# Block sums of a Fourier transform's matrix, made by accumulating DMAs in place of VectorE

## The chip, the cores and the metric

The kernel runs on one core of a Trainium2 chip. The metric is the device time in microseconds of one execution. Before the change, three runs took 742.9, 743.92 and 747.85 us; their median is 743.92 us.

The core has a matrix engine (TensorE, PE in the profile, with its weight loads as PEld), a vector engine (VectorE, DVE), an engine for activation functions (ScalarE, ACT), a programmable engine (GpSimd, POOL) and SyncE (SP), which here only issues transfers. The engines run side by side, each through its own list of instructions in order, and wait for each other by semaphores. 16 DMA engines move data between the memory of the chip (HBM) and the core's own memory (SBUF, 128 partitions). TensorE accumulates in PSUM.

## The reference

`x` has 2048 rows (the sequence) of 512 values. The output mixes two branches of it by a gate per row:

```python
g = sigmoid((x * gate_w).sum(-1, keepdims=True))
# A: real part of a Fourier transform over both axes
a = x @ dft_hid_re.T;  b = x @ dft_hid_im.T
A = dft_seq_re @ a - dft_seq_im @ b
# B: gated feed-forward layer, F = 1376
B = (silu(x @ w1) * (x @ w3)) @ w2
out = g * A + (1 - g) * B
```

All is float32. The Fourier matrices come as inputs, as any matrix would.

## The kernel before

**Products.** A float32 product is three passes on TensorE: each operand is split into a high part (rounded) and a low part (the rest), and high x high, high x low and low x high are accumulated (`mm3`, L85). The split is made by `split` (L76): ScalarE writes the high part by a copy (L77), VectorE the low part by a subtraction (L83). Each operand that comes from memory or from a sum passes through it.

**Stages.** The feed-forward branch comes first, up to 339 us of the profile. Then the transform along the sequence, Z = (C x) by blocks, up to 652 us, which spills Z to HBM. Then the product with the hidden matrix, the gate and the sum.

**The sequence transform** is a product of 2 x 2 blocks by 2 x 2 blocks, made in seven products and some sums (Winograd's form of Strassen's algorithm). The fixed operand `A` is made from `x` once (`load_a`, L414 to L433): blocks and sums of blocks, split, in `A1` and `A2`. The moving operand is the matrix C, which is streamed from HBM (`cc`): for each of four column groups `tb` and each of eight pairs `p` of row tiles, four blocks of 128 x 512 floats, which the host has laid side by side. C needs four blocks as they are and sums of blocks.

The work is a list of 64 steps `(tb, g, p)` (L435). For each `tb` there are eight steps with g = 0, of four products each, and then eight with g = 1, of three products each. Each product of a step is six matmuls of 128 x 512. In a step:

- `load_c(n + 4)` (L438) asks SyncE for the blocks of the step four later. For g = 0 it loads blocks 0 and 1 into a wide buffer `cu` and block 2 into half of a wide buffer `cv`; for g = 1 blocks 2 and 3 into `cu`, block 1 into half of `cv`.
- `sums_c(n + 2)` makes two sums on VectorE, 128 x 512 each. For g = 0: T1 = block 2 - block 0 (L469), T2 = block 1 - T1 (L470). T2 stays in a half buffer, because the same pair p needs it again in g = 1. For g = 1: block 1 - block 2 (L472), and block 3 - T2 (L473).
- `prep_c1(n + 2)` splits the wide buffer `cu`, `prep_c2(n + 2)` the sums (T1 and T2 for g = 0, the last sum for g = 1), into `zo`, of which there are four buffers.
- Six or eight accumulators in PSUM are carried over the eight steps; after the last of them VectorE adds them up (L556 to L590) and the result is spilled.

The wide buffers (`wide`, L73) come from one pool `f4` of 13, which loads of all stages share. SyncE's queue issues all these loads in order, each when its buffer has been read to the end. The lines of code call the helpers in an order written out by hand; the framework's scheduler then sets each engine's order from the dependences, so that the lists of the engines are not always in the order of the code. The first steps' loads and preparations are called from the end of the feed-forward stage (`xacts`, L500 to L517).

After the transform, the last two of the four tiles of the hidden matrix are split with their sign turned (`load_d`, `neg=True`, L79).

Of the kernel before, what the change touches and what calls it, by code (L numbers as in the profile page):

```python
# [7 lines left out]
F32 = mybir.dt.float32  # L8
F32R = mybir.dt.float32r
AF = mybir.ActivationFunctionType  # L10
ALU = mybir.AluOpType

P = 128
# [15 lines left out]
def fnet_swiglu_gate_kernel(  # L29
# [11 lines left out]
):  # L41
    """A float32 product is three passes: each operand v is split exactly into
    hi = v rounded to 12 significant bits and lo = v - hi, and hi*hi + hi*lo +
    lo*hi is accumulated in float32.

    The gate and up products are one 2x2x2 block product (gate | up weights by
    halves of D by two token blocks) in the seven products of Winograd's form of
    Strassen's algorithm, and so is the transform along the sequence (halves of
    D by halves of the sequence by re | im)."""
    nc = tc.nc  # L50
# [24 lines left out]

    def split(hi, lo, src, neg=False):  # L76
        nc.scalar.activation(hi, src, AF.Copy, scale=-1.0 if neg else 1.0)  # L77
        if neg:
            nc.vector.scalar_tensor_tensor(  # L79
                lo, src, -1.0, hi.bitcast(F32), op0=ALU.mult, op1=ALU.subtract  # L80
            )
        else:
            nc.vector.tensor_sub(lo, src, hi.bitcast(F32))  # L83

# [11 lines left out]

# [1 line left out]
    XO, ST = {}, {}  # L98

    def load_xo(g, t, j):  # L100
        """Half j of the staged operands t of token blocks 2g and 2g+1."""
        if g not in ST:
            ST[g] = [[wide(f"xs{g}_{q}_{i}") for i in range(4)] for q in range(2)]
            XO[g] = [xo.tile([P, 2, 7, 512], F32R, tag="xo", name=f"xo{g}_{q}") for q in range(2)]
        for q in range(2):
            nc.sync.dma_start(ST[g][q][t][:, j * 512 : (j + 1) * 512],
                              xt[g, q, :, t * 1024 + j * 512 : t * 1024 + (j + 1) * 512])

    # moving operands B11 B21 B22 T1 T2 T3 -T4 and where they are staged
    AT = {"B12": (0, 0), "B11": (0, 1), "B21": (1, 0), "B22": (1, 1),  # L110
# [29 lines left out]
    def prep_wa(i, lo=0, hi=3):  # L140
        """A11 A12 A22"""
        if lo == 0:
            WA[i] = wo.tile([P, 2, 3, 256], F32R, tag="wa", name=f"wa{i}", bufs=LOOK + 1)
        t = WA[i]
        split(t[:, 0, lo:hi].rearrange("p a n -> p (a n)"),
              t[:, 1, lo:hi].rearrange("p a n -> p (a n)"),
              WS[i][:, lo:hi].rearrange("p a n -> p (a n)"))

    def prep_wb(i, part=None):
        """S1 S2 S3 S4"""  # L150
        if part != 1:
            w = WS.pop(i)
            u = wo.tile([P, 4, 256], F32, tag="wu", name=f"wu{i}", bufs=1)
            nc.vector.tensor_add(u[:, 0], w[:, 3], w[:, 2])
            nc.vector.tensor_sub(u[:, 1], u[:, 0], w[:, 0])
            nc.vector.tensor_sub(u[:, 2], w[:, 0], w[:, 3])
            nc.vector.tensor_sub(u[:, 3], w[:, 1], u[:, 1])
            WB[i] = u
        if part != 0:
            u = WB[i]  # L160
            t = wo.tile([P, 2, 4, 256], F32R, tag="wb", name=f"wb{i}")
            split(t[:, 0].rearrange("p a n -> p (a n)"), t[:, 1].rearrange("p a n -> p (a n)"),
                  u.rearrange("p a n -> p (a n)"))
            WB[i] = t
# [19 lines left out]
    def first2(i):  # L184
        """the gate of the first block is P1 + P2"""
        y = bank(4 + i % 2, f"Y{i}")
        prod(y, i, 1, 1, True)
        s1 = G[i][1]
        nc.vector.tensor_add(s1, s1, y)
        nc.scalar.activation(s1, s1, AF.Silu)  # L190
# [90 lines left out]
    def plain(b12, a21):  # L281
        """The first chunk in eight products: they need no sums."""
        c = {}

        def half(i, j, w, x, start):
            if start:
                c[i, j] = bank((0, 4, 6, 7)[2 * i + j], f"C{i}{j}")
            for r in range(2):
                sl = slice(r * P, (r + 1) * P)
                mm3(c[i, j], w(0, sl), w(1, sl), x(r, 0), x(r, 1), start and r == 0,  # L290
                    not start and r == 1)

        def wa(k):
            return lambda h, sl: WA[0][:, h, k, sl]

        def xb(k):
            return lambda q, h: XO[0][q][:, h, k, :]

        w21 = lambda h, sl: a21[:, h, sl]
        x12 = lambda q, h: b12[:, h, q * 512 : (q + 1) * 512]  # L300
        s1 = tp.tile([P, 512], F32, tag="s1", name="s1_0", bufs=LOOK + 2)
        g1 = tp.tile([P, 512], F32, tag="g1", name="g1_0")
        h = wide("h0")
        H[0] = h
        yield half(0, 0, wa(0), xb(0), True)
        yield half(1, 0, w21, xb(0), True)
        half(0, 0, wa(1), xb(1), False)
        nc.scalar.activation(s1, c[0, 0], AF.Silu)
        yield half(1, 0, wa(2), xb(1), False)
        nc.vector.tensor_mul(h[:, :512], s1, c[1, 0])  # L310
        half(0, 1, wa(0), x12, True)
        yield half(1, 1, w21, x12, True)
        half(0, 1, wa(1), xb(2), False)
        nc.scalar.activation(g1, c[0, 1], AF.Silu)
        half(1, 1, wa(2), xb(2), False)
        yield nc.vector.tensor_mul(h[:, 512:], g1, c[1, 1])
# [91 lines left out]

# [1 line left out]
    # rows d (halves) by [re | im] columns t, reduced over s (halves)  # L410
    a2_cm, a2 = pool("a2", 1, "left")
# [8 lines left out]
    def load_a(p):  # L420
        """A11 S1 S2 S4 | A12 A22 S3 of the rows s of tiles p and p + 8."""
        r = wide(f"xr{p}").rearrange("p (a n) -> p a n", a=4)
        m = wide(f"xm{p}").rearrange("p (a n) -> p a n", a=4)
        nc.sync.dma_start(flat(r), xn[p])
        a21, a11, a12, a22 = (r[:, i] for i in range(4))
        nc.vector.tensor_add(m[:, 0], a21, a22)
        nc.vector.tensor_sub(m[:, 1], m[:, 0], a11)
        nc.vector.tensor_sub(m[:, 2], a12, m[:, 1])
        nc.vector.tensor_sub(m[:, 3], a11, a21)
# [5 lines left out]
    steps = [(tb, g, p) for tb in range(NTB) for g in range(2) for p in range(NG)]  # L435
    RAW, T2, ZO = {}, {}, {}

    def load_c(n):  # L438
        if n >= len(steps):
            return  # L440
        tb, g, p = steps[n]
        u, v = wide(f"cu{n}"), wide(f"cv{n}")
        src = cc[tb, p]
        if g == 0:
            nc.sync.dma_start(u, src[:, :1024])
            nc.sync.dma_start(v[:, :512], src[:, 1024:1536])
        else:
            nc.sync.dma_start(u, src[:, 1024:])
            nc.sync.dma_start(v[:, :512], src[:, 512:1024])
        RAW[n] = u, v  # L450

# [8 lines left out]

    def sums_c(n):
        if n >= len(steps):
            return
        tb, g, p = steps[n]
        u, v = RAW[n]
        if g == 0:
            b11, b22 = u[:, :512], u[:, 512:]
            T2[tb, p] = v[:, 512:] if p % 2 == 0 else RAW[n - 1][1][:, :512]
            nc.vector.tensor_sub(v[:, :512], v[:, :512], b11)  # L469
            nc.vector.tensor_sub(T2[tb, p], b22, v[:, :512])  # L470
        else:
            nc.vector.tensor_sub(u[:, :512], v[:, :512], u[:, :512])  # L472
            nc.vector.tensor_sub(v[:, 512:], u[:, 512:], T2.pop((tb, p)))  # L473

    def prep_c1(n):
        if n < len(steps):
            zsplit(n, 0, RAW[n][0])

    def prep_c2(n):
        if n >= len(steps):  # L480
            return
        tb, g, p = steps[n]
        v = RAW[n][1]
        if g == 1:
            zsplit(n, 1, v[:, 512:])
        elif p % 2 == 0:
            zsplit(n, 1, v)
        else:
            zsplit(n, 1, v[:, :512], T2[tb, p])

# [10 lines left out]
    for p in range(NG):  # L501
        xacts[p].append(lambda p=p: load_a(p))
    xacts[7].append(lambda: load_c(0))
    xacts[8].append(lambda: load_c(1))
    xacts[9].append(lambda: prep_c1(0))
    xacts[10].append(lambda: sums_c(0))
    xacts[10].append(lambda: prep_c2(0))
# [5 lines left out]
    prep_c1(1)  # L513
    sums_c(1)
    prep_c2(1)
    load_c(2)
    load_c(3)  # L517

# [5 lines left out]
    def fourier_step(n):  # L524
        tb, g, p = steps[n]
        fst, lst = p == 0, p == NG - 1
        load_c(n + 4)
        sums_c(n + 2)
        z0, z1 = ZO.pop((n, 0)), ZO.pop((n, 1))
# [64 lines left out]

# [1 line left out]
    DW, ZY = [], {}  # L596

    def load_d(q):
        r = wide(f"dr{q}")
        nc.sync.dma_start(r, dd[q])  # L600
        t = yd.tile([P, 2, 1024], F32R, tag=f"d{q}", name=f"d{q}")
        split(t[:, 0], t[:, 1], r, neg=q >= 2)
        DW.append(t)
# [113 lines left out]
```

## Time and profile before

| | before |
|---|---|
| median of three runs | 743.92 us |
| span of the profiled execution, first to last instruction | 742.8 us |
| matmuls | 3196 |
| sequence transform, matmuls | 339 to 652 us |
| DMA moved | 112.5 MB, mean 151 GB/s |
| HBM read, written | 95.16 MB, 16.78 MB |
| transfers of the moving operand | 64 of 512 KB and 64 of 256 KB |

The time outside the span isn't listed for the profiled execution; its span lies at the lowest of the three times.

How to read the lines that follow. A row of a group of instructions names line, engine and operation, then output <- inputs with their shape and the count, then the busy time in us and the mean ns of one, and behind the second bar the idle time of that engine just before these instructions with what ended it. A row of a wait says which engine's instruction waited for what, with the total in us, the number of times and the longest. A row of a tile gives the shortest, median and longest duration in ns, and the time of the first and the last one. In the timeline a row begins with its start and length in us.

### The profile page before, as it was taken

What the parts mean: (1) busy time and instruction counts of PE and PEld (TensorE: products, weight loads), DVE (VectorE), ACT (ScalarE), POOL (GpSimd) and SP (SyncE); (2) the same over time, 40 slices, a digit from 0 to 9 for tenths busy, and PEclk for the clock granted to TensorE, in tenths of its full rate; (3) what the DMA queues carried; (4) which work ended last, traced back from release to release, by engine and by line L of the source; (5) the groups of instructions that cost most, each with busy time, mean ns of one, the idle gap of its engine ahead of it and who ended that gap; (6) DMA issues with size and microseconds to landing.
All of it is one profiled execution on the core that took longest, in us unless ns stands there. A gap on an engine that the chain in (4) does not pass through costs nothing.

```text
span 742.8 us, 8637 instructions
## 1 busy us (share of the span) xinstructions
PE 731.3 (98%) x3196; PEld 597.6 (80%) x3196; DVE 541.0 (73%) x793; ACT 336.5 (45%) x455; POOL 0.2 (0%) x4
## 2 busy tenths in 40 slices
PE   8999999999999999999999899999999999999998
PEld 5788888888888888888887688878887788888886
DVE  6997788792777668994986887779776978834331
ACT  6755463554554436753443344344343445523320
POOL 0000000000000000000000000000000000000000
PEclk9999999999999999999999999999999999999999
DMA  7112126532013003608656554655465647963331
GB/s 268 51 65 85 57 75 248 163 124 114 30 56 114 1 28 113 210 32 313 225 172 224 197 182 146 220 189 203 153 213 172 217 163 244 350 241 114 114 107 63
DMA packets 40378, 112.50 MB, mean 151 GB/s; under 512 B 4368, under 2 KB 4752, under 8 KB 40336
## 3 DMA queue, kind: packets, MB, share of 16 engines
q1 hardware_dynamic: 38032, 107.89, 42.1%
q10 hardware_dynamic: 2304, 4.06, 1.5%
q8 instruction: 25, 0.41, 0.2%
q14 instruction: 17, 0.14, 0.1%
HBM read 95.16 MB, written 16.78 MB: 151 GB/s over the span
## 4 chain that ended last, share of the span: by engine, by line
PE 82%; DVE 8%; DMA 8%; issue 1%; ACT 1%; SPq 0%; DVEq 0%; ACTq 0%
PE P L87 26%; PE acc L87 16%; PE X L87 16%; PE y L87 12%; PE Z L87 8%; DMA cv<-cc 7%; DVE zo L83 5%; PE Y L87 4%; PE C L87 1%; DVE cv L469 1%; DMA xs<-xt 1%; DVE cv L470 1%; DVE zu L583 1%; DMA cu<-cc 1%; DVE zu L584 0%
## 5 line engine op out<-in xcount | busy, mean ns | idle before, releaser
L87 PE MATMUL P<-zo,a 128*128 128x512 f32 x1344 | 307.7, 390 | 5.6 <-DVE zo L83 4.8
L87 PEld LDWEIGHTS P<-zo,a 128*128 128x128 f32 x1344 | 251.4, 188 | 61.8 <-DVE zo L83 7.6
L87 PE MATMUL acc<-w2o,ho 128*128 128x512 f32 x528 | 120.1, 389 | 0.0
L77 ACT ACTIVATE zo<-cu 128x1024 fp32r<-128x1024 f32 x64 | 67.9, 1060 | 111.9 <-PE P L87 82.8
L87 PEld LDWEIGHTS acc<-w2o,ho 128*128 128x128 f32 x528 | 99.1, 188 | 20.7
L87 PE MATMUL X<-xo,wb 128*128 128x512 f32 x378 | 93.8, 390 | 0.0
L87 PE MATMUL y<-d,zy 128*128 128x512 f32 x384 | 87.2, 389 | 0.0
L87 PEld LDWEIGHTS y<-d,zy 128*128 128x128 f32 x384 | 72.1, 188 | 15.0
L77 ACT ACTIVATE zo<-cv 128x512 fp32r<-128x512 f32 (+1 forms) x80 | 56.2, 715 | 61.7 <-PE P L87 50.8
L87 PEld LDWEIGHTS X<-xo,wb 128*128 128x128 f32 x378 | 70.6, 188 | 15.6 <-DVE u L206 0.5
L83 DVE TENSOR_TENSOR zo<-cu,zo 128x1024 fp32r<-128x1024 f32 x64 | 78.2, 1222 | 2.6 <-ACT zo L77 2.5
L83 DVE TENSOR_TENSOR zo<-cv,zo 128x512 fp32r<-128x512 f32 (+1 forms) x80 | 62.3, 796 | 4.0 <-ACT zo L77 4.0
L83 DVE TENSOR_TENSOR zy<-zr,zy 128x1024 fp32r<-128x1024 f32 x16 | 19.5, 1225 | 40.6 <-ACT zy L77 36.3
L469 DVE TENSOR_TENSOR cv<-cv,cu 128x512 f32<-128x512 f32 x32 | 21.8, 694 | 33.6 <-DMA cv<-cc 33.6
L77 ACT ACTIVATE zy<-zr 128x1024 fp32r<-128x1024 f32 x16 | 16.8, 1056 | 44.7 <-PE y L87 43.1
L77 ACT ACTIVATE wa<-ws 128x768 fp32r<-128x768 f32 (+2 forms) x23 | 18.8, 818 | 33.6 <-PE Z L87 32.0
L87 PE MATMUL X<-xo,wa 128*128 128x512 f32 x126 | 32.7, 391 | 0.0
L87 PE MATMUL Y<-xo,wa 128*128 128x512 f32 x126 | 32.5, 389 | 0.0
L87 PE MATMUL Z<-xo,wb 128*128 128x512 f32 x126 | 32.3, 389 | 0.0
L87 PE MATMUL Z<-xo,wa 128*128 128x512 f32 x126 | 32.2, 389 | 0.0
L83 DVE TENSOR_TENSOR wb<-wu,wb 128x1024 fp32r<-128x1024 f32 x21 | 25.7, 1225 | 8.2 <-ACT wb L77 8.1
L472 DVE TENSOR_TENSOR cu<-cv,cu 128x512 f32<-128x512 f32 x32 | 22.1, 691 | 12.6 <-DMA cv<-cc 11.1
(84 smaller groups left out, 661.2 us busy)
## 6 DMA issues: line engine op xcount, KB each, us to landing
cu<-cc SPq DMA_DIRECT2D x64, 512.0 KB, 4.5
cv<-cc SPq DMA_DIRECT2D x64, 256.0 KB, 3.8
ws<-w SPq DMA_DIRECT2D x21, 512.0 KB, 3.2
zr<-zsp SPq DMA_DIRECT2D x16, 512.0 KB, 6.0
w2r<-w SPq DMA_DIRECT2D x10, 512.0 KB, 4.1
xs<-xt SPq DMA_DIRECT2D x16, 256.0 KB, 5.3
sr<-xs SPq DMA_DIRECT2D x8, 512.0 KB, 4.2
bsp<-b SPq DMA_DIRECT2D x8, 512.0 KB, 3.0
```

Source lines behind the costliest of these rows:

```text
L77: nc.scalar.activation(hi, src, AF.Copy, scale=-1.0 if neg else 1.0)
L83: nc.vector.tensor_sub(lo, src, hi.bitcast(F32))
L87: nc.tensor.matmul(ps, u, v, start=first and n == 0, stop=last and n == 2, skip_group_check=chain)
L469: nc.vector.tensor_sub(v[:, :512], v[:, :512], b11)
L470: nc.vector.tensor_sub(T2[tb, p], b22, v[:, :512])
L472: nc.vector.tensor_sub(u[:, :512], v[:, :512], u[:, :512])
L583: nc.vector.tensor_add(u4[:, r], u4[:, r], U["P7"][r])
```

## The change

The four sums of a pair p are no longer made by VectorE. GpSimd's queue issues DMAs that add what they read to what lies at their destination (`add_dma`). The sums are all additions now: T1 = block 2 + block 0, T2 = block 1 + T1, then block 2 + block 1 and block 3 + T2. That is the transform with the sign of two blocks turned; the sums of `A` in `load_a` follow, and the hidden matrix is split without turning a sign.

- T1 and T2 get wide buffers of their own, each shared by an even and an odd p (`pairs`). For g = 0 SyncE loads blocks 0 and 1 into `cu`, block 2 into T1 and block 1 into T2. Then an accumulating DMA adds block 0 from HBM to T1, and another adds T1 to T2 from SBUF to SBUF; this second one is called a step later.
- For g = 1 SyncE loads blocks 2 and 3 into `cu`, and that is all. Accumulating DMAs add block 1 to the first half of `cu`, and block 3 to T2, which has lain there since g = 0.
- `add_c(n + 4)` issues these just behind `load_c(n + 4)`. The third step's load and adds are called earlier than before, in the last chunk of the stage ahead.
- What the host hands over is the same.

```diff
@@ load_a
-        nc.vector.tensor_add(m[:, 0], a21, a22)
-        nc.vector.tensor_sub(m[:, 1], m[:, 0], a11)
-        nc.vector.tensor_sub(m[:, 2], a12, m[:, 1])
+        nc.vector.tensor_sub(m[:, 0], a22, a21)
+        for d, v, w in ((1, m[:, 0], a11), (2, a12, m[:, 1])):
+            nc.vector.scalar_tensor_tensor(m[:, d], v, -1.0, w, op0=ALU.mult, op1=ALU.subtract)
@@ new
+    def add_dma(dst, src):
+        nc.gpsimd.dma_start(dst, src, accum_op=ALU.add)
+
+    def pairs(tb, p, src):
+        if p % 2 == 0:
+            T1[tb, p // 2] = wide(f"t1_{tb}_{p}")
+            T2[tb, p // 2] = wide(f"t2_{tb}_{p}")
+        h = slice(p % 2 * 512, p % 2 * 512 + 512)
+        nc.sync.dma_start(T1[tb, p // 2][:, h], src[:, 1024:1536])
+        nc.sync.dma_start(T2[tb, p // 2][:, h], src[:, 512:1024])
@@ load_c
-        u, v = wide(f"cu{n}"), wide(f"cv{n}")
+        u = RAW[n] = wide(f"cu{n}")
         src = cc[tb, p]
         if g == 0:
             nc.sync.dma_start(u, src[:, :1024])
-            nc.sync.dma_start(v[:, :512], src[:, 1024:1536])
+            pairs(tb, p, src)
         else:
             nc.sync.dma_start(u, src[:, 1024:])
-            nc.sync.dma_start(v[:, :512], src[:, 512:1024])
@@ in place of sums_c
-        if g == 0:
-            b11, b22 = u[:, :512], u[:, 512:]
-            T2[tb, p] = v[:, 512:] if p % 2 == 0 else RAW[n - 1][1][:, :512]
-            nc.vector.tensor_sub(v[:, :512], v[:, :512], b11)
-            nc.vector.tensor_sub(T2[tb, p], b22, v[:, :512])
-        else:
-            nc.vector.tensor_sub(u[:, :512], v[:, :512], u[:, :512])
-            nc.vector.tensor_sub(v[:, 512:], u[:, 512:], T2.pop((tb, p)))
+    def add_c(n):
+        if n < len(steps):
+            tb, g, p = steps[n]
+            src = cc[tb, p]
+            if g == 0:
+                add_dma(half(T1, tb, p), src[:, :512])
+            else:
+                add_dma(RAW[n][:, :512], src[:, 512:1024])
+                add_dma(half(T2, tb, p), src[:, 1536:])
+        if 0 < n <= len(steps) and steps[n - 1][1] == 0:
+            tb, g, p = steps[n - 1]
+            add_dma(half(T2, tb, p), half(T1, tb, p))
@@ prep_c2
-        v = RAW[n][1]
-        if g == 1:
-            zsplit(n, 1, v[:, 512:])
-        elif p % 2 == 0:
-            zsplit(n, 1, v)
+        if g == 0:
+            zsplit(n, 1, half(T1, tb, p), half(T2, tb, p))
         else:
-            zsplit(n, 1, v[:, :512], T2[tb, p])
+            zsplit(n, 1, half(T2, tb, p))
@@ first steps, called from the stage ahead
     xacts[7].append(lambda: load_c(0))
+    xacts[7].append(lambda: add_c(0))
     xacts[8].append(lambda: load_c(1))
+    xacts[8].append(lambda: add_c(1))
     xacts[9].append(lambda: prep_c1(0))
-    xacts[10].append(lambda: sums_c(0))
+    xacts[10].append(lambda: load_c(2))
+    xacts[10].append(lambda: add_c(2))
     xacts[10].append(lambda: prep_c2(0))
...
     prep_c1(1)
-    sums_c(1)
+    load_c(3)
+    add_c(3)
     prep_c2(1)
-    load_c(2)
-    load_c(3)
@@ fourier_step
         load_c(n + 4)
-        sums_c(n + 2)
+        add_c(n + 4)
@@ load_d
-        split(t[:, 0], t[:, 1], r, neg=q >= 2)
+        split(t[:, 0], t[:, 1], r)
```

More of the change, by code (lines that the diff above doesn't have):

```diff
@@ L74, in wide, with split @@
         return f4.tile([P, 1024], F32, tag="f4", name=name)
[L76 to L81, printed above, removed]
-        else:
-            nc.vector.tensor_sub(lo, src, hi.bitcast(F32))
+    def split(hi, lo, src):
+        nc.scalar.activation(hi, src, AF.Copy)
+        nc.vector.tensor_sub(lo, src, hi.bitcast(F32))
     def mm3(ps, ah, al, bh, bl, first, last, chain=False):
@@ L435, in fnet_swiglu_gate_kernel, with half @@
     steps = [(tb, g, p) for tb in range(NTB) for g in range(2) for p in range(NG)]
-    RAW, T2, ZO = {}, {}, {}
+    RAW, T1, T2, ZO = {}, {}, {}, {}
+    def add_dma(dst, src):
[7 more added lines that the diff above has]
+        nc.sync.dma_start(T2[tb, p // 2][:, h], src[:, 512:1024])
+    def half(t, tb, p):
+        return t[tb, p // 2][:, p % 2 * 512 : p % 2 * 512 + 512]
     def load_c(n):
@@ L445, in load_c @@
             nc.sync.dma_start(u, src[:, :1024])
-            nc.sync.dma_start(v[:, :512], src[:, 1024:1536])
+            pairs(tb, p, src)
         else:
             nc.sync.dma_start(u, src[:, 1024:])
-            nc.sync.dma_start(v[:, :512], src[:, 512:1024])
-        RAW[n] = u, v
+    def add_c(n):
[10 more added lines that the diff above has]
+            add_dma(half(T2, tb, p), half(T1, tb, p))
     def zsplit(n, i, *srcs):
@@ L459, in zsplit @@
         ZO[n, i] = t
[L461 to L465, printed above, removed]
-        if g == 0:
-            b11, b22 = u[:, :512], u[:, 512:]
-            T2[tb, p] = v[:, 512:] if p % 2 == 0 else RAW[n - 1][1][:, :512]
[L469 to L473, printed above, removed]
     def prep_c1(n):
         if n < len(steps):
-            zsplit(n, 0, RAW[n][0])
+            zsplit(n, 0, RAW.pop(n))
     def prep_c2(n):
```

## The prediction

> **What bounds the kernel now.** I read the busy shares first, then the windows of the stage that the change touches, then its waits, then the DMA side.
>
> The busy shares of the page:
>
> ```profile
> span 742.8 us, 8637 instructions
> ...
> PE 731.3 (98%) x3196; PEld 597.6 (80%) x3196; DVE 541.0 (73%) x793; ACT 336.5 (45%) x455; POOL 0.2 (0%) x4
> ```
>
> TensorE has work for 98% of the span; VectorE is busy, but not the bound, and GpSimd does nothing. The change lies in the sequence transform. Its matmuls run from 338.9 to 652.1 us (first and last row of the chain in order of time that belong to it, and the row after):
>
> ```profile
> 338.89 10.94 PE P L87 x48
> ...
> 577.66 74.41 PE P L87 x327
> 652.07 87.05 PE y L87 x384
> ```
>
> Its loads and splits run from 309.4 to about 645 (instructions on the buffer `cu`):
>
> ```profile
> L83 DVE TENSOR_TENSOR zo<-cu,zo x64: 1216/1221/1243, 322.2 to 644.8; 128x1024 fp32r<-128x1024 f32 x64
> L445 SPq DMA_DIRECT2D cu<-cc x32: 327/328/737, 309.4 to 581.2; - x32
> ```
>
> The windows view gives both stretches, and the stretch where the DMA engines were fullest (columns: stretch, length, then busy time and count for PE, PEld, DVE, ACT, POOL, then granted clock, mean busy share of the 16 DMA engines, GB/s):
>
> ```profile
> 309.00:645.00 336.00, 330.40 (x1446) 270.26 (x1445) 269.81 (x361) 149.19 (x181) 0.00 (x0) 1.00 0.58 198
> 631.00:650.00 19.00, 19.00 (x85) 15.73 (x85) 16.44 (x20) 11.37 (x14) 0.00 (x0) 1.00 0.91 347
> 339.00:652.00 313.00, 307.40 (x1345) 251.24 (x1344) 248.72 (x326) 132.38 (x156) 0.00 (x0) 1.00 0.61 210
> ```
>
> In the stage PE is idle for 313.0 - 307.4 = 5.6 us. That is all that any relief of VectorE can give back here. Who ends these gaps, by the waits of PE and of its weight loads in the stretch 338 to 653 (columns: total us, times, longest):
>
> ```profile
> PE P L87 <- DVE zo L83: 4.8, 6, 1.2
> PE P L87 <- DVE zu L584: 0.8, 3, 0.3
> ```
>
> The late thing is the low part of a split matrix block, made on VectorE. VectorE in turn waits for a load, and the load for a buffer (waits of all engines, then SyncE's queue):
>
> ```profile
> DVE cv L469 <- DMA cv<-cc: 33.6, 16, 7.7
> ```
>
> ```profile
> SPq L449 <- DVE zo L83: 68.1, 30, 4.6
> SPq L446 <- DVE zo L83: 61.7, 24, 6.5
> ```
>
> One such gap in the timeline:
>
> ```profile
> 413.07 0.69 DVE L469 TENSOR_TENSOR cv<-cv,cu 128x512 f32<-128x512 f32 x1 [3.12 <-DMA cv<-cc]
> ...
> 413.68 1.22 DVE L83 TENSOR_TENSOR zo<-cu,zo 128x1024 fp32r<-128x1024 f32 x1
> 414.81 0.68 DVE L83 TENSOR_TENSOR zo<-cv,zo 128x512 fp32r<-128x512 f32 x1
> 414.93 0.33 SPq L446 DMA_DIRECT2D cv<-cc  x1
> 414.95 5.77 PEld L87 LDWEIGHTS P<-zo,a 128*128 128x128 f32 x26 [1.59 <-DVE zo L83]
> ```
>
> VectorE sat 3.12 us until the load had landed, then did the sum and two splits, and TensorE's weight load, 1.59 us late, started as the last split ended. So the short gaps come where VectorE and the buffers are late together.
>
> **What is removed.** Each pair of blocks costs four sums. Two rows from the page, two from the groups by line:
>
> ```profile
> L469 DVE TENSOR_TENSOR cv<-cv,cu 128x512 f32<-128x512 f32 x32 | 21.8, 694 | 33.6 <-DMA cv<-cc 33.6
> ...
> L472 DVE TENSOR_TENSOR cu<-cv,cu 128x512 f32<-128x512 f32 x32 | 22.1, 691 | 12.6 <-DMA cv<-cc 11.1
> ```
>
> ```profile
> L473 DVE TENSOR_TENSOR cv<-cu,cv 128x512 f32<-128x512 f32 x32 | 22.1, 690 | 7.2 <-DMA cu<-cc 6.7
> L470 DVE TENSOR_TENSOR cv<-cu,cv 128x512 f32<-128x512 f32 x32 | 22.0, 691 | 0.3
> ```
>
> 128 instructions of 0.69 us leave VectorE: 88 us of its 269.8 in the stretch. On the path that sets the end this is worth at most the 5.6 us of gaps, because TensorE covers the rest.
>
> **What is small.** In the first half of the steps the second operand is now always split in two pieces, where for the 16 even steps it was one wide piece:
>
> ```profile
> L77 ACT ACTIVATE zo<-cv x80: 610/633/1064, 326.4 to 643.9; 128x512 fp32r<-128x512 f32 x64, 128x1024 fp32r<-128x1024 f32 x16
> L83 DVE TENSOR_TENSOR zo<-cv,zo x80: 682/688/1230, 327.5 to 646.0; 128x512 fp32r<-128x512 f32 x64, 128x1024 fp32r<-128x1024 f32 x16
> ```
>
> That is 16 times 2 x 633 - 1064 = 0.2 us on ACT and 16 times 2 x 688 - 1230 = 0.15 us on VectorE, 3.2 and 2.3 us under TensorE's cover; if the cover went, at most 5.5 us. The turned signs replace additions by subtractions, or by a two-operation form, of the same size: nothing. SyncE issues as many loads as before, 128: a step of the first half has three in place of two, one of the second half one in place of two, with the same bytes.
>
> **What is added.** 128 accumulating DMAs of 128 x 512 floats (262,144 bytes) on GpSimd's queue, 33.6 MB in all. 96 read the matrix, so 25.2 MB more come from HBM; 32 add one block sum in SBUF to another. No accumulating transfer and no DMA of GpSimd's stands in the trace, so its price has to be bounded.
>
> First the room. In the stretch 309 to 645 the DMA engines are busy for 0.58 x 336 = 195 us at 198 GB/s, which is 66.5 MB, or 341 GB/s while busy. Room up to a full share: 336 - 195 = 141 us, or 141 / 128 = 1.10 us for each accumulating DMA. At the fullest that a row shows, 0.91, it is 0.91 x 336 - 195 = 111 us, 0.87 us for each.
>
> Then the price of one, in time of all 16 engines. A plain transfer of this size takes 262,144 B / 341 GB/s = 0.77 us. The lower end is this price: the second read hides. The upper end is twice it, 1.54 us: an accumulate reads two blocks and writes one, and if reading sets the pace, it takes twice as long. In between, three passes over the data in place of two would give 1.15 us. I take 1.15: it counts every pass of the data once, and I have no row that says that reading alone sets the pace.
>
> The sum by that price: 195 + 128 x 1.15 = 342 us of DMA work. At a share of 0.91 this takes 342 / 0.91 = 376 us, where the stretch had 336: 40 us more. The old gaps are inside the 336, so nothing is to be subtracted. 742.8 + 40 = 783 us for the profiled span. The three runs took 742.9 to 747.85 us; the span lies at the lowest of them and 1.1 us under their median of 743.92, so I forecast 784.
>
> The ends by the same sum: at 0.77 us, 195 + 98 = 293 us, 0.87 of the stretch, and nothing is lost; at 1.15 us and a full share 342 us, 6 us lost; at 1.54 us 392 us, 56 us lost at a full share and 392 / 0.91 - 336 = 95 us at 0.91.
>
> A rule that speaks against this change: the Trainium skill, DMA: Bandwidth & Descriptors, section Issuing engines are not separate DMA queues, says that DMAs of ScalarE, SyncE and GpSimd run on the same 16 engines and interleave. No row of this trace shows two of these queues under load together; if GpSimd's transfers had engines of their own, the sum would be no loss and at most the 5.6 us of gain.
>
> **The new waits.** Landing times, and what an issue costs its queue:
>
> ```profile
> cu<-cc SPq DMA_DIRECT2D x64, 512.0 KB, 4.5
> cv<-cc SPq DMA_DIRECT2D x64, 256.0 KB, 3.8
> ```
>
> ```profile
> L446 SPq DMA_DIRECT2D cv<-cc x32: 327/328/1516, 310.7 to 581.8; - x32
> ...
> DMA to landing us min/median/max: 3.0/3.8/8.7
> ```
>
> A block of the first half is now a chain: load, add, add, three landings. At the median it takes 4.5 + 3.8 + 3.8 = 12.1 us. A step is 24 products of about 0.228 us (row below), 5.5 us, or 18 products, 4.1 us. Loads are asked for four steps ahead, 16 to 22 us, so 12.1 us fit; three landings at the worst row's 8.7 us, 26 us, don't.
>
> ```profile
> 421.42 58.79 PE L87 MATMUL P<-zo,a 128*128 128x512 f32 x258 [0.28 <-DVE zu L584]
> ```
>
> GpSimd's queue is in order. Adding the first block sum to the second waits on it for the first to land, and the adds of the next pair of steps stand behind. An add for the second half waits for VectorE's split of the same buffer, with the next blocks' adds behind it. What waits in turn are ScalarE's splits of these blocks, then VectorE's, then TensorE. Before, the second half loaded two buffers a step; now one, the other lying there already. So with the same 13 buffers the loads may run further ahead, which speaks for the latency being hidden, and for engine time being what is left.
>
> **The rivals.**
>
> Hidden: the accumulates cost about the plain price. The DMA engines then stand at 0.87, below the 0.91 that was reached without a stall, and VectorE's relief takes away some of the gaps. 743.9 - 5.6 = 738.3 us if all go; 742 if the later chain leaves most of them. For it: the 141 us of room, and the gaps ending on VectorE. Against it: any price above 0.87 to 1.10 us ends it. This is the one on the other side; the price per transfer decides, at 1.10 us.
>
> Twice: reading sets the pace, 1.54 us each, 56 to 95 us lost, 800 to 839 us. For it: nothing in the trace shows a second read to be free. Against: the rows show no engine's read and write sides apart. The Trainium skill, Collectives: The Full Stack, section The bandwidth ceiling, says that an add in the DMA path needs two source reads on one ring and so halves the rate; no run here shows that.
>
> GpSimd's queue: the issue on it, not the transfer, sets the pace. A block of 512 columns takes 8 x 5.5 + 8 x 4.1 = 77 us and has 32 accumulates and, in the first half, up to 8 exposed landings of 3.8 us, 30 us. That leaves 47 / 32 = 1.45 us for each issue. SyncE's usual 0.33 us is far below, its longest 1.52 us just above: 32 x 1.52 + 30 = 79 us, 2 us over a block, 8 us in four, 752. An issue of 3 us would give 126 us a block and 940 us; nothing in the trace excludes it, since GpSimd issued nothing.
>
> **How the numbers follow.** Three passes (about 752 to 799, forecast 784): 0.37. Hidden, with the small loss of 6 us at a full share (737 to 751): 0.33. Twice (800 to 840): 0.20. GpSimd's queue, a little over the limit: 0.04 inside the range, and 0.06 far above. The forecast's own range is 750 to 799; with cases of both signs the range is 737 to 839, with some 0.1 left out, nearly all above. About 1% (7.4 us) is what a measurement of this kernel can tell from no change. Faster by over 1% needs below 736.5, which is more than the 5.6 us of gaps: 0.05, for gaps that the records don't show. Within 1%: the rest of the hidden case, 0.28. Slower: the other three, 0.67.
>
> **What would show it.** The four sum groups gone and VectorE near 455 us; a new queue with 33.6 MB and a share of 16 engines: its share of the span over 128 is the price, and 1.15 us each would be 147 us of 784, about 19%. A DMA share near 0.9 throughout the stage; PE idle for some 40 us, the wait before it ending on ScalarE's or VectorE's splits, and these on accumulating DMAs; clock unchanged at 1.00. The forecast is wrong if that queue's share gives 0.8 us or less each (hidden) or 1.5 (twice), or if the DMA engines are far below 0.9 while GpSimd's queue is never empty (issue or landing sets the pace).

## The result, and the profile after

The changed kernel takes 792.36 us (median of four runs, 787.92 to 795.74) against 745.13 us for the kernel before, run beside it (four runs, 742.9 to 747.85). The ratio is 1.063, with a 95% interval of 1.060 to 1.066. The forecast was 784 us with a range of 737 to 839. The profiled execution took 792.24 us, with a span of 790.4.

The page of the changed kernel: busy shares, two rows of the 40 slices, and the DMA queues (packets, MB, share of the 16 engines over the span).

```profile
span 790.4 us, 8944 instructions
...
PE 747.8 (95%) x3196; PEld 604.7 (77%) x3196; DVE 465.2 (59%) x681; ACT 333.7 (42%) x471; POOL 112.6 (14%) x132
...
PEclk9999999999999999998899999989999899999999
DMA  7111146440130036899999999999999999973321
...
q1 hardware_dynamic: 38032, 107.89, 38.9%
q0 software_dynamic: 18432, 33.56, 24.5%
```

VectorE has lost 541.0 - 465.2 = 75.8 us of work, as the sums are gone. A new queue has moved 33.56 MB, and its packets took 24.5% of 790.4 us, 193.7 us; for one of the 128 accumulating DMAs that is 1.51 us of all 16 engines. From about 336 us, where the stage's matmuls begin, to about 690 the DMA row stands at 9. The packets of SyncE's queue (q1) took 38.9% x 790.4 = 307 us; before, for the same 107.89 MB, they took 42.1% x 742.8 = 313 us:

```profile
q1 hardware_dynamic: 38032, 107.89, 42.1%
```

So a packet isn't recorded as longer because the engines are fuller, and the shares can be added up as work. The windows view of the same stretch as before, as far as it now reaches:

```profile
309.00:690.00 381.00, 344.96 (x1436) 275.67 (x1436) 194.04 (x248) 145.09 (x195) 112.38 (x128) 0.96 1.01 264
```

The DMA share is 1.01 over 381 us, where it was 0.58 over 336. (A value above 1 means that the recorded times of packets on one engine overlap, so 1 is no sharp end.) The granted clock is 0.96, where it was 1.00. Two rows for the stage's matmuls, before and after, from the groups of PE by line: busy, mean ns of one, and the idle time before them.

```profile
L87 PE MATMUL P<-zo,a 128*128 128x512 f32 x1344 | 307.7, 390 | 5.6 <-DVE zo L83 4.8 <-DVE zu L584 0.8
```

```profile
L82 PE MATMUL P<-zo,a 128*128 128x512 f32 x1344 | 324.2, 402 | 35.5 <-ACT zo L77 17.4 <-DVE zu L593 11.3 <-DVE zo L78 6.6
```

Idle time grew by 29.9 us, and the same 1344 matmuls took 16.5 us longer: 46.4 of the 47.6 us by which the span grew. A clock of 0.96 over 381 us is 15 us of clock lost, so the slower matmuls are the clock. The waits of all engines after, those that lead from TensorE to the DMAs:

```profile
ACT zo L77 <- DMA t<-t: 75.2, 20, 9.2
...
ACT zo L77 <- DMA cu<-cc: 33.3, 9, 5.8
...
ACT zo L77 <- DMA t<-cc: 23.9, 9, 8.0
```

TensorE waits for ScalarE's split, and ScalarE for a landing, most of all for the last link of the chain, T2 + T1. The 11.3 us that end on VectorE's line 593, a sum at the end of a block, lead there too: before the wait that ends at 612.35 us, VectorE had itself stood 6.77 us for ScalarE's part of a split, and ScalarE 7.72 us for T2 + T1 to land. The landings themselves (issues on SyncE's and GpSimd's queue, median us to landing):

```profile
cu<-cc SPq DMA_DIRECT2D x64, 512.0 KB, 8.3
t<-cc SPq DMA_DIRECT2D x64, 256.0 KB, 8.7
t<-cc POOLq DMA_DIRECT2D x64, 256.0 KB, 7.4
...
t<-t POOLq DMA_DIRECT2D x32, 256.0 KB, 7.1
```

A load that landed in 4.5 us before now takes 8.3. Two readings are possible. The DMA engines are full, and the landings are late because of that ("engine time"). Or the chain of three landings and GpSimd's queue, in order, are what is slow, and the high share only goes along with it ("queue and chain").

### The profile page after: what moved, and what is told of

Same layout as the page of the kernel before. It is cut to its first block, busy times and chain, and to the rows that moved or that the text cites. A ratio compares the mean times of both kernels' runs of the same rounds, so it can differ in the third digit from the quotient of the medians.

```text
span 790.4 us, 8944 instructions
## 1 busy us (share of the span) xinstructions
PE 747.8 (95%) x3196; PEld 604.7 (77%) x3196; DVE 465.2 (59%) x681; ACT 333.7 (42%) x471; POOL 112.6 (14%) x132
## 3 DMA queue, kind: packets, MB, share of 16 engines
q1 hardware_dynamic: 38032, 107.89, 38.9%
q0 software_dynamic: 18432, 33.56, 24.5%
HBM read 120.32 MB, written 16.78 MB: 173 GB/s over the span
## 4 chain that ended last, share of the span: by engine, by line
PE 48%; DMA 27%; issue 12%; POOL 6%; DVE 5%; ACT 1%; POOLq 0%; SPq 0%; DVEq 0%; ACTq 0%
DMA t<-cc 15%; PE X L82 15%; PE y L82 11%; PE acc L82 8%; PE Z L82 7%; DMA cu<-cc 5%; POOL t L436 5%; DMA t<-t 4%; PE Y L82 4%; PE P L82 2%; DMA zr<-zsp 2%; POOL cu L436 2%; DVE a L78 1%; PE C L82 1%; ACT zo L77 1%
## 5 line engine op out<-in xcount | busy, mean ns | idle before, releaser
L82 PE MATMUL P<-zo,a 128*128 128x512 f32 x1344 | 324.2, 402 | 35.5 <-ACT zo L77 17.4
L82 PEld LDWEIGHTS P<-zo,a 128*128 128x128 f32 x1344 | 258.8, 194 | 100.8 <-ACT zo L77 21.7
L436 POOL DMA_DIRECT2D t<-cc x64 | 60.4, 964 | 421.0 <-ACT a L77 315.4
L78 DVE TENSOR_TENSOR zo<-t,zo 128x512 fp32r<-128x512 f32 x96 | 64.7, 687 | 92.0 <-ACT zo L77 92.0
L77 ACT ACTIVATE zo<-t 128x512 fp32r<-128x512 f32 x96 | 58.9, 625 | 118.4 <-DMA t<-t 75.2
L436 POOL DMA_DIRECT2D t<-t x32 | 28.6, 893 | 95.1 <-DMA t<-cc 57.1
L436 POOL DMA_DIRECT2D cu<-cc x32 | 27.9, 872 | 50.9 <-issue 46.6
```

Source lines behind the costliest of these rows:

```text
L77: nc.scalar.activation(hi, src, AF.Copy)
L82: nc.tensor.matmul(ps, u, v, start=first and n == 0, stop=last and n == 2, skip_group_check=chain)
L436: nc.gpsimd.dma_start(dst, src, accum_op=ALU.add)
```

## The experiments

The medians of the kernel before on the same chips were 744 to 746 us. "In the stage" below is the stretch from 309 us to the end of the splits.

**Plain copies in place of the accumulating ones.** The order of instructions is that of the changed kernel on every engine.

```diff
-        nc.gpsimd.dma_start(dst, src, accum_op=ALU.add)
+        nc.gpsimd.dma_start(dst, src)
```

> The changed kernel with plain copies on GpSimd's queue in place of the 128 accumulating ones: same number, same blocks, same waits, and no sum is made. Engine time (an accumulate takes 193.7 / 128 = 1.51 us of all 16 engines, a plain one about 0.77, and the engines are full): 195 + 98 = 293 us fit into the stage, 738 to 750 us, and the software queue's share falls from 24.5% to about 13%. Queue and chain (GpSimd waits in order for landings, three in a row): the waits stay, 770 to 792 us.

Measured: 741.77 us, one run, beside 746.01 for the kernel before. Windows of the stage, the stage's matmuls and the queue:

```profile
309.00:640.00 331.00, 327.95 (x1441) 269.87 (x1440) 194.81 (x248) 149.45 (x197) 69.11 (x128) 1.00 0.92 308
```

```profile
L82 PE MATMUL P<-zo,a 128*128 128x512 f32 x1344 | 306.6, 390 | 3.1 <-ACT zo L77 2.3 <-DVE zo L78 0.7
```

```profile
q0 software_dynamic: 10240, 33.56, 14.2%
```

With the same number of DMAs, the same bytes written and the same order of waits, but without the addition and the second read, 50 us are gone. One plain copy takes 14.2% x 740.0 / 128 = 0.82 us. The DMA share is 0.92, and TensorE idles for 3.1 us. HBM isn't the limit: as much is read from it as in the changed kernel (120.32 MB), and in the stage 308 GB/s are moved where the changed kernel moved 264. Queue and chain aren't cleared by this run alone: a plain copy takes GpSimd 0.54 us to issue, an accumulate 0.87, the queue has 10240 packets in place of 18432, and the chain's landings are shorter too, 6.3 + 6.7 + 5.5 = 18.5 us at the medians.

**Half and three quarters of the columns.** The accumulating DMAs keep their number and their order (but for two early in GpSimd's queue that change places) and move fewer bytes.

```diff
-        nc.gpsimd.dma_start(dst, src, accum_op=ALU.add)
+        nc.gpsimd.dma_start(dst[:, :256], src[:, :256], accum_op=ALU.add)
```

> The changed kernel with each accumulating DMA cut to its first 256 of 512 columns, so that half of each sum is left out: same number, same waits, half the bytes. Engine time: 195 + 128 x 0.76 = 292 us, fits, 738 to 752 us. Queue and chain: 128 issues and all waits remain and landings get only a little shorter, 768 to 790 us.

> The changed kernel with each accumulating DMA cut to 384 of its 512 columns, so that a quarter of each sum is left out; the order of every engine is the same. Engine time: between 0.87 us (256 columns) and 1.51 us (512) lies 1.19 us; work in the stage 304 us of the run with plain copies + 128 x (1.19 - 0.82) = 352 us, at the full share of 1.01 348 us where that run took 331: 742 + 17 = 759 us, 750 to 765. Queue and chain: the waits are nearly those of the changed kernel, 770 to 785 us.

Measured: 742.23 us with 256 columns (one run, beside 746.01), 767.73 us with 384 (ratio 1.032 to the kernel before, 1.028 to 1.037). The queue of each, and the window of the stage with 256 columns:

```profile
q0 software_dynamic: 18432, 16.79, 15.0%
```

```profile
q0 software_dynamic: 18432, 25.17, 20.4%
```

```profile
309.00:640.00 331.00, 326.47 (x1436) 268.99 (x1435) 194.33 (x248) 148.83 (x197) 112.67 (x128) 1.00 0.95 256
```

Both have the 18432 packets of the changed kernel, and GpSimd takes as long to issue (with 256 columns 112.67 / 128 = 0.88 us each). So neither the issue nor the number of packets makes the loss. One DMA takes 15.0% x 740.5 / 128 = 0.87 us with 256 columns, 20.4% x 765.1 / 128 = 1.22 with 384, and 1.51 with 512: it goes mostly by the bytes, half of them costing 0.58 as much, and not by the number of DMAs or packets. The time with 384 columns lies between the two expectations, 3 us above the range of the one and 2 under that of the other, so it decides less than the half did. Its queue took 156 us of all engines, less than the 168 us of the run with 96 accumulates below, and it cost as much.

**Only the first half's DMAs accumulate, only the second half's, or all but T2 + T1.** The others are plain copies; again the order of all engines is that of the changed kernel.

```diff
-    def add_dma(dst, src):
-        nc.gpsimd.dma_start(dst, src, accum_op=ALU.add)
+    def add_dma(dst, src, **kw):
+        nc.gpsimd.dma_start(dst, src, **kw)
...
-                add_dma(half(T1, tb, p), src[:, :512])
+                add_dma(half(T1, tb, p), src[:, :512], accum_op=ALU.add)
...
-            add_dma(half(T2, tb, p), half(T1, tb, p))
+            add_dma(half(T2, tb, p), half(T1, tb, p), accum_op=ALU.add)
```

> The changed kernel with its 64 accumulating DMAs of the first half (T1 and T2, the chain of three landings) as they are, and plain copies in place of the 64 of the second half, whose sums are left out; same order on every engine. Engine time: 304 + 64 x 0.69 = 348 us of work, 345 us at a share of 1.01, 331 before: 756 us, 745 to 762, and the same as with only the second half accumulating. Queue and chain: the chain of three is whole, 775 to 790 us.

> The changed kernel with only the 64 accumulating DMAs of the second half, and plain copies in place of the chain's 64 in the first half, whose sums are left out; same order on every engine. Engine time: 756 us, 745 to 762, as with only the first half accumulating. Queue and chain: no chain of accumulates, 740 to 746 us.

> The changed kernel with plain copies in place of only the 32 DMAs that add T1 to T2 in SBUF, so that this sum is left out; 96 accumulate, same order on every engine. Engine time: 304 + 96 x 0.69 = 370 us of work, 367 us at a share of 1.01, 331 before: 742 + 36 = 778 us, 765 to 785. Against the run with this sum on VectorE (796.6 us with 96 accumulates) it tells what VectorE's waiting in its own order cost there. Queue and chain: the waits of the chain stay, 780 to 792 us.

Measured, with the ratio to the kernel before and its interval, and the share and the idle time of the stage's matmuls from the profiles:

| accumulating, of 128 | us | ratio | DMA share in the stage | PE idle, us |
|---|---|---|---|---|
| none | 741.77 | one run | 0.92 | 3.1 |
| 64, second half | 746.47 | 1.002 (1.000 to 1.004) | 0.99 | 7.0 |
| 64, first half | 749.42 | 1.007 (1.005 to 1.010) | 0.98 | 9.2 |
| 96, all but T2 + T1 | 765.44 | 1.028 (1.023 to 1.032) | 1.01 | 17.1 |
| 128 | 792.36 | 1.063 (1.060 to 1.066) | 1.01 | 35.5 |

The share and the idle time are those of one execution each. For the first half's 64 that was the slowest of six, 753.95 us, so its 9.2 us are on the high side.

64 accumulates bring the share to about 1, with 5 to 8 us lost against the one run with none; each 32 more then cost 16 to 19 and 27 us. Which half accumulates matters by 3 us only, though the intervals don't overlap. With the first half's the chain is as long as in the changed kernel, 7.5 + 8.2 + 7.4 = 23.1 us at the medians, and 8 us are lost where the changed kernel loses 51, so queue and chain as the main cause falls. The 3 us needn't be the chain: a step of the first half also loads four blocks in 5.5 us, one of the second half two in 4.1. And the last 32 are the chain's last link, so part of the 27 us may be the chain's; no run separates that. Engine time had the shape, not the sizes: it gave 756, 756 and 778 us, and the loss sets in later and grows faster. If a plain copy takes 0.82 us, the queues' shares leave 1.39 to 1.48 us for an accumulate in these three mixed runs. That plain copies and accumulates fill the engines in the proportion of 0.82 to 1.51 and that 1.01 is the end is thus good for the place of the limit within some 10 us, no better.

**A source in SBUF.** Blocks 0 and 3 are added from `cu`, where they lie already.

```diff
-                add_dma(half(T1, tb, p), src[:, :512])
+                add_dma(half(T1, tb, p), RAW[n][:, :512])
...
-                add_dma(half(T2, tb, p), src[:, 1536:])
+                add_dma(half(T2, tb, p), RAW[n][:, 512:])
```

> The changed kernel with blocks 0 and 3 added from the buffer cu in SBUF, where they lie already, in place of HBM: 64 of the 96 accumulates that read HBM read SBUF, 16.8 MB less from HBM. Engine time by passes over the data: the engines move the same, 780 to 795 us. If HBM reads are what costs: 745 to 770 us. Queue and chain: the adds wait for cu as well, 788 to 800 us.

Measured: 838.97 us, one run, beside a median of 746.34: slower than any theory had it. The queue, and the largest waits of SyncE's queue in this stage:

```profile
q0 software_dynamic: 18432, 33.56, 22.8%
```

```profile
SPq L460 <- DMA t<-cu: 76.5, 18, 10.1
...
SPq L460 <- DMA t<-t: 39.9, 8, 7.3
```

One accumulate takes 22.8% x 837.2 / 128 = 1.49 us, as with HBM for a source, while the reads from HBM fell from 120.32 to 103.55 MB; so reading HBM isn't what makes it dear. What is new is that a load waits until an accumulate has read the buffer that it is to fill. Here the queue and the buffers do cost: the DMA share in the stage falls to 0.92, and TensorE idles for 66.2 us.

**DMAs beside the kernel before.** Two DMAs in each step, into four buffers that no product reads, accumulating or plain.

```diff
+            nc.gpsimd.tensor_copy(x[:, :1], z[:, 1, :1].bitcast(F32))
+            nc.gpsimd.dma_start(x, cc[tb, p][:, k * 512 : k * 512 + 512], accum_op=ALU.add)
```

> The kernel before, with its sums on VectorE, and beside them two accumulating DMAs of 128 x 512 from HBM in each of the 64 steps, into four buffers that nothing else reads, paced by a small copy on GpSimd from the step's operand. Nobody waits for their landing but the next use of the same buffer, two steps later. Engine time: 195 + 193 = 388 us of DMA work where the stretch had 336, 785 to 800 us. Queue and chain: no product waits for these, 744 to 752 us.

> As the run with the accumulating DMAs beside the kernel before, but plain copies. Engine time: 195 + 98 = 293 us, 0.87 of the stretch, 744 to 752 us. Queue and chain: 744 to 752 us as well. It shows what the four extra DMA buffers, the small copies and the issue on GpSimd cost without the second read.

Measured: 823.85 us accumulating, 787.44 plain, one run each, beside 746.01. The control lost 41 us, against both theories, so the pair doesn't tell what it should. The small copy that paces the DMAs reads the split operand, and it made that buffer's next user wait (the kernel with plain copies):

```profile
ACT zo L77 <- POOL xe L520: 14.8, 5, 4.9
```

That covers only a part of the 41 us. The loads landed later, 5.8 and 5.0 us at the median where the kernel before has 4.5 and 3.8, and VectorE's sums wait for them; that this is the rest wasn't tested. The queues' shares give 13.5% x 785.6 / 128 = 0.83 us for a plain copy and 24.0% x 822.1 / 128 = 1.54 us for an accumulate, the prices of the other runs, and 36 us lie between the two.

**T2 + T1 on VectorE.** 96 accumulating DMAs remain.

```diff
-            add_dma(half(T2, tb, p), half(T1, tb, p))
+            nc.vector.tensor_add(half(T2, tb, p), half(T2, tb, p), half(T1, tb, p))
```

> The changed kernel with the sum T2 + T1 (32 DMAs from SBUF to SBUF) back on VectorE as 32 additions; 96 accumulating DMAs remain and the chain of three landings becomes one of two. Engine time: 195 + 96 x 1.51 = 340 us where 336 were, 4 us over, 744 to 760 us. Queue and chain: 64 accumulates of the second half and 32 of the first still pass GpSimd's queue in order, but its waits for a landing go, 748 to 770 us.

Measured: 796.64 us, ratio 1.069 (1.067 to 1.072), far over both. The run with as many accumulates and T2 + T1 as a plain copy took 765.4. VectorE's waits and a piece of its timeline:

```profile
DVE t L476 <- DMA t<-cc: 115.5, 22, 13.1
```

```profile
484.42 0.68 DVE L78 TENSOR_TENSOR zo<-t,zo 128x512 fp32r<-128x512 f32 x1
498.20 0.69 DVE L476 TENSOR_TENSOR t<-t,t 128x512 f32<-128x512 f32 x1 [13.10 <-DMA t<-cc]
498.81 1.22 DVE L78 TENSOR_TENSOR zo<-cu,zo 128x1024 fp32r<-128x1024 f32 x1
499.95 0.68 DVE L78 TENSOR_TENSOR zo<-t,zo 128x512 fp32r<-128x512 f32 x1
```

The addition stands on VectorE in front of the splits and waits there, 13.10 us, for the accumulate into T1, which GpSimd had issued at 491.47 us; the split of another buffer follows within 0.6 us. In these two runs a wait on GpSimd holds up transfers that aren't due yet; the same wait on VectorE holds up splits that are.

**A smaller dose.** The second half's sums by 64 accumulating DMAs, the first half's on VectorE, and block 1 not loaded a second time; and the same with only block 1 added by DMA (32).

```diff
-            if g == 0:
-                add_dma(half(T1, tb, p), src[:, :512])
-            else:
+            if g == 1:
                 add_dma(RAW[n][:, :512], src[:, 512:1024])
                 add_dma(half(T2, tb, p), src[:, 1536:])
...
+        if g == 0:
+            nc.vector.tensor_add(t1, t1, u[:, :512])
+            nc.vector.tensor_add(t2, t1, u[:, 512:])
```

> The changed kernel with the two sums of the first half on VectorE (T1 in place, T2 = T1 + block 1 from cu, so that block 1 isn't loaded a second time) and the two of the second half by 64 accumulating DMAs. Engine time: 195 - 32 x 0.77 + 64 x 1.51 = 267 us, 0.80 of the stretch, no loss, 738 to 748 us. Queue and chain: no DMA waits for another accumulate's landing within the first half, 742 to 760 us.

> As the run with the second half's sums alone by DMA, but only block 1 is added to cu by DMA (32 accumulates) and the other three sums are on VectorE. Engine time: 195 - 25 + 48 = 219 us, 0.65 of the stretch. As one transfer and its buffer are gone from the second half's steps, the old gaps of 5.6 us may shrink: 738 to 745 us by both theories; it tells whether a small dose of the change gains over the kernel before.

Measured: with 64, 737.88 us against 746.34, ratio 0.989 (0.987 to 0.990): some 1% faster than the kernel before. With 32, 767.6 us, ratio 1.029 (1.026 to 1.031), which neither theory expected. The windows of the stage and its matmuls with 64:

```profile
309.00:637.00 328.00, 327.91 (x1446) 270.89 (x1445) 233.24 (x314) 151.09 (x198) 55.90 (x64) 1.00 0.84 234
```

```profile
L82 PE MATMUL P<-zo,a 128*128 128x512 f32 x1344 | 305.4, 390 | 0.1
```

TensorE has no gap left: 5.5 us of idle time and 2.3 us of matmul time less than before. With 32 accumulates the DMA share is 0.64, so the engines aren't the cause there. VectorE's waits again:

```profile
DVE t L478 <- DMA cu<-cc: 63.4, 22, 5.2
```

```profile
L82 PE MATMUL P<-zo,a 128*128 128x512 f32 x1344 | 314.6, 396 | 20.2 <-DVE zu L572 13.3 <-DVE zo L78 6.9
```

It is the addition of block 3 to T2, the one sum that the faster kernel gives to GpSimd and this one to VectorE. It waits in VectorE's order for a load, with the sums at the end of a block and the splits behind it. The chain of work that ended last runs in a circle there (start, us, what):

```profile
451.45 1.15 DVE zo L78
452.61 6.39 DMA cu<-cc
459.78 1.14 DVE zo L78
460.94 5.05 DMA cu<-cc
```

A split ends and frees a buffer, the next load is issued at once and lands at 459.00, the addition runs at 459.09, and the next split stands behind it. The place on VectorE alone doesn't make this: the kernel before has its sums there too, and its wait for the same load came to 6.7 us in all (L473), against 63.4 here. What made the loads late here no run separates.

## Why the prediction was right, point by point

**The direction and the cause were right.** The DMA engines became the bound: with the same waits and plain copies the loss is gone, and it comes back with the number and the width of the accumulates, while the queue, the issue and the order stay.

**The price was mis-sized.** The step that took 1.15 us for an accumulate failed. It measured 1.49 to 1.55 us in the runs in which 64 or more accumulate and the queue holds nothing else, the upper end of the bound (1.54); with 32 and emptier engines it was 7.2% x 764.7 / 32 = 1.72. A plain copy on this queue takes 0.82. By the prediction's own sign, 1.5 us or more, this is the rival "twice", and the price in the forecast was the wrong one. The time still lies under that rival's 800 to 840 us, which were worked out with 1.54 us and shares of 1.00 and 0.91. The reason given for 1.15, that every pass of the data counts once, has nothing in the runs for it; the rule of the Trainium skill (Collectives: The Full Stack, section The bandwidth ceiling), stated there for the adding step of collectives, two source reads and so half the rate, fits the ratio 1.51 / 0.82 = 1.84. That the second read is what takes the time, and not the adding, no run here separates.

**The ceiling was mis-sized too, the other way.** The forecast let the engines fill up to 0.91, the fullest row; they went to 1.01 over 381 us. With the measured price and ceiling the sum is (195 + 194) / 1.01 = 385 us where 336 were, 49 us, and the span grew by 47.6. At the forecast's own values it was 40. The measured price with the forecast's ceiling gives 389 / 0.91 - 336 = 91 us, the measured ceiling with the forecast's price 3 us. The two errors nearly cancelled: that the time came within 8 us of the forecast is luck, though its direction isn't.

**Where the loss shows.** Forecast: some 40 us of idle TensorE, at a clock of 1.00. Measured: 35.5 us of idle time, 30 more than before, and 16.5 us in slower matmuls, the clock at 0.96; the prediction had put the clock at nothing. Where the DMA engines set the length, slower matmuls may only fill time that would have been idle, so these are two parts of one loss rather than two causes. 24.0 of the 35.5 us end on splits, as written, and the splits on landings; the 11.3 us behind sums at the end of a block weren't foreseen.

**GpSimd's queue.** An issue takes 0.87 us (medians 866 to 878 ns), between the two SyncE rows that bounded it and under the limit of 1.45. It set no pace: with 256 columns in place of 512 an issue takes as long, and nothing was lost.

**The chain.** Three landings were 12.1 us at the old medians (11.4, if the first is the 256 KB load that it is); at the new ones they are 8.7 + 7.4 + 7.1 = 23.2 us, over the 16 to 22 us of lead. The prediction kept the old landing times beside fuller engines. By the two runs with 64 accumulates the chain is worth 3 us at most there.

**VectorE's relief.** 75.8 us less busy, where 86 were forecast: the sums overlap their neighbours in time (in the prediction's timeline one takes 0.69 us and the next instruction starts 0.61 us after it), so that the busy time of the engine is less than the sum of its instructions. What relief can buy was bounded too low, at the 5.6 us of gaps: with 64 accumulates and two of the four sums on VectorE the gain is 8.5 us (7 to 10 by the interval). In the profile 5.5 us of it are the gaps and 2.3 us shorter matmul time, which the bound took as fixed; why it is shorter isn't shown. With plain copies and no sums at all the one run is 4.2 us under its neighbour, no more than runs of the kernel before differ by.

## What to carry to other kernels

Price an accumulating DMA at about twice a plain one of its size, and add up the DMA engines' time of that stage, not of the kernel, before moving sums to it; here there was room for 64, not for 128. Look at what stands behind each wait on the engine that gets it: a sum that waits for a transfer is cheap on a queue with time in hand, and dear on the engine that also makes the next operands. In the kernel before, with loads that came in time, the same sums on VectorE cost little. A run with the same instructions in the same order and one property taken away told more here than moving the work to another engine, which changed orders along with it.

## What the runs showed of the hardware that wasn't expected

A gap in TensorE's work slows the matmuls behind it. Weight loads in the timeline of the changed kernel, and the windows around the gap that ends at 612.35 us:

```profile
601.35 5.09 PEld L82 LDWEIGHTS P<-zo,a 128*128 128x128 f32 x23 [1.07 <-DVE zo L78]
612.35 0.93 PEld L82 LDWEIGHTS P<-zo,a 128*128 128x128 f32 x3 [5.91 <-DVE zu L593]
```

```profile
606.00:616.00 10.00, 4.51 (x13) 3.18 (x12) 5.59 (x10) 3.35 (x5) 2.71 (x5) 0.77 0.99 252
616.00:626.00 10.00, 10.00 (x41) 8.15 (x40) 6.24 (x8) 3.62 (x6) 2.63 (x4) 0.89 1.04 263
626.00:636.00 10.00, 10.00 (x46) 8.29 (x45) 4.77 (x6) 3.56 (x6) 2.86 (x4) 1.00 1.07 309
```

In the window with the end of a wait of 5.91 us the granted clock was 0.77, in the next 0.89; in the ten microseconds from 616 TensorE was busy throughout and did 41 matmuls, in the next ten 46. In the whole stage slower matmuls came to the 16.5 us above. The Trainium skill, TensorE: Matmul & The Clock Gate, section HAM oscillation, advises against idle gaps of over some 3.4 us for this reason. The traces agree: the kernel before, whose longest wait of PE in this stage was 1.2 us, kept a clock of 1.00, and so did the runs with plain copies and with 256 columns, with 1.7 and 2.1 us; in the run with the second half's 64 accumulates the longest was 3.2 us and the clock 0.99.
